# Loading, turning and masking the first two chunks of a windowed attention with FFN in another way

## The chip, the cores and the metric

The kernel runs on one core of a Trainium2 chip. The metric is device time in microseconds (us) of one execution; the time before is 178.18 us, the median of 3 runs (177.92 to 179.19). One further execution was recorded by the hardware profiler, and every duration below is from it.

The engines are named as in the profile: PE (TensorE, matrix products; PEld is its weight load), DVE (VectorE), ACT (ScalarE), POOL (GpSimd) and SP (SyncE, which here only issues DMAs). Each works through its own instructions in order and waits for others by semaphores. 16 DMA engines move data; SP and Pool each feed them through a queue of their own.

## The reference, cut to what matters

```python
scores = q @ k.T / sqrt(64)               # q, k, v: (4 batches, 8 heads, 768 tokens, 64)
keep   = is_sink | in_window              # first 4 tokens, or the 128 tokens up to this one
a      = softmax(where(keep, scores, -1e9))
x      = (a @ v), heads side by side      # (3072, 512)
h      = maximum(maximum(x @ w1, x @ w2), x @ w3)     # w1, w2, w3: (512, 768)
out    = h @ w_out                        # (3072, 512), float32
```

All inputs are float32; the kernel computes its products in bf16.

## The kernel before, in words

**Chunks.** The 3072 tokens are cut into 12 chunks of 256 (three to a batch). For each chunk: load K, Q, V; cast to bf16; turn K and Q so that the head dimension lies on the partitions; scores, exponentials, mask, sink scores; attention times V; normalise; turn the result; three FFN products with a running maximum; the output product; store. Heads are taken in four pairs (`p` = 0 to 3), the two heads of a pair are `a` = 0, 1. A group `g` is half of the heads, that is, two pairs. A token's number in its chunk is split as `(p i)`, so that a partition holds two tokens that follow each other; `n` is the half of the chunk of 128 keys.

**Order.** The order of instructions is written out by hand: each Python call appends its instructions to the engines' queues in the order of the calls (L408 to L613). The first chunks are written one by one, from chunk 3 on a loop runs (L561). The loop is full of FFN matmuls; the first 20 us, before the weights have landed, are not, and they are what the change rewrites.

**Loads.** `load` (L72) moves one of K, Q, V of a chunk from float32 in memory to a float32 tile (`k_raw`, `q_raw`, `v_raw`), in pieces of 512 bytes. At the start SP issues K and Q of chunk 0 in two halves of heads each, then V of chunk 0, then K, Q and V of chunk 1 (L131 to L134). `load_w` (L197) moves an FFN weight from float32 to bf16 through Pool's queue; W1 and W2 in halves of the model dimension, W3 in halves of the hidden one. Later loads are gated: a one-element copy on Pool writes the destination once something has landed, and the DMA waits for that copy (`after`, L485). Chunk 2's K and Q hang on the last half of W2, the output weight on W3.

**Turning.** `cast_qk` (L89) casts a group to bf16, and `turn` (L102) transposes its four 128x128 blocks on PE against the identity into one PSUM bank, which ACT (Q) or DVE (K of chunk 0) copies to `qT` and `kT`.

**Masks.** `masks` (L157) builds `msk` with 1 where a key is seen and 0 elsewhere; `msk0` is the same for the first chunk of a batch, with the sink tokens kept. `expo` (L232) takes the exponential of two PSUM banks on ACT and multiplies the pair by the mask on DVE (L239).

**Values.** `cast_v` (L97) casts a quarter of V to `vb`, which holds a column of ones as well, so that `av` (L284) yields the sum of the exponentials in a 65th column. `sink_k` and `sink_v` pick the four sink tokens' K and V out of a batch's first chunk, and `sink_score` (L241) scores against them.

**Filler and banks.** `warm(n)` (L143) issues n matmuls of 512 columns whose result nobody reads. PSUM has eight banks, which all PE results share in turn; a new result waits until the one that held its bank before has been read.

**First stretch.** Chunk 0's groups are cast by DVE (K) and ACT (Q), turned and scored; V's quarters are cast two by DVE and two by Pool; W1's two halves are issued by Pool behind these casts. K of chunk 1 is cast by ACT, Q by Pool, and both are turned between the `av` calls of chunk 0. Then chunk 0's result is turned (`xpose`), chunk 1 scored, and `ffn_h_half` (L351) does half a contraction of the first FFN product with each half of W1, mixed with `av` of chunk 1.

Of the kernel before, what the change touches and what calls it, by code (L numbers as in the profile page):

```python
# [9 lines left out]
F32 = mybir.dt.float32  # L10
# [6 lines left out]
def kernel(  # L17
# [31 lines left out]
    with tc.manual_schedule():  # L49
# [22 lines left out]
        def load(ci, what="kqv", gate=None, parts=1, only=None, eng=None):  # L72
# [4 lines left out]
            for w in what:  # L77
# [5 lines left out]
                for g in range(parts) if only is None else (only,):  # L83
# [3 lines left out]
                            .rearrange("h (p i) d -> p h (i d)", i=2))  # L87

        def cast_qk(ci, w, g, eng):  # L89
# [12 lines left out]
        def turn(ci, w, g, eng=None):  # L102

            pt = bank([128, 4, 128], BF16, "pt")
            x = bfs[ci, w]
            for i in range(4):
                y = x[:, 2 * g + i // 2, i % 2]
                nc.tensor.transpose(pt[:, i], y.rearrange("s a d -> s (a d)"), ident)  # L108
            if w == "q":
                nc.scalar.copy(  # L110
                    qT[ci % RING][:, 2 * g:2 * g + 2].rearrange("q p i n r -> q (p i) (n r)"), pt)
            else:
                (nc.scalar.copy if eng is nc.scalar else nc.vector.tensor_copy)(
                    kT[ci % RING][:, :, 2 * g:2 * g + 2].rearrange("q n p i r -> q n (p i) r"),
                    pt.rearrange("q x (n r) -> q n x r", r=64))
# [17 lines left out]
        load(0, "v")  # L133
        load(1)  # L134

# [18 lines left out]
        msk = const.tile([128, 2, 4, 128], BF16, name="msk")  # L154
        msk0 = const.tile([128, 2, 3, 128], BF16, name="msk0")

        def masks():  # L157
# [52 lines left out]

        def score(ci, pairs):
            b, c = divmod(ci, CPB)
            kc, qc = kT[ci % RING], qT[ci % RING]
            lo = 0 if c else 1
            sts = {p: [bank([128, 4, 128], F32, "st") for a in range(2)] for p in pairs}
            for p in pairs:
                st = sts[p]
                for s, x, n, q0, q1 in ((0, kT[(ci - 1) % RING], 1, 0, 1), (1, kc, 0, 0, 2),
# [3 lines left out]
                    for a in range(2):  # L222
# [4 lines left out]
                            rhs=qc[hp, p, :, q0:q1].rearrange("q i n r -> q n i r"),  # L227
                            start=True, stop=True)
                e = work.tile([128, 2, 4, 128], BF16, tag="e", bufs=2 * NP, name="e_sb")
                es[ci, p] = e, st  # L230

# [9 lines left out]
        def sink_score(ci):  # L241
# [4 lines left out]
            for p in range(NP):  # L246
# [4 lines left out]
                    start=True, stop=True, tile_position=(0, 32 * p))  # L251
            e = work.tile([128, 2, 128], BF16, tag="e_sink", bufs=2, name="e_sink")
            nc.scalar.activation(e, st, AF.Exp, scale=scale)  # L253
            es[ci, "sink"] = e

# [13 lines left out]
        def av_open(ci, pairs=range(NP)):  # L269
# [3 lines left out]
            if c:  # L273
                for t in range(2):
                    for p in pairs:
                        hp = slice(32 * p, 32 * p + 32)
                        nc.tensor.matmul(  # L277
                            os_[ci, p][:, t], lhsT=es[ci, "sink"][hp, t], rhs=vs[b % 2][hp],
                            start=(t == 0), stop=False, skip_group_check=True,
# [129 lines left out]
        masks()  # L409
        sink_init()  # L410
        cast_qk(0, "k", 0, nc.vector)
        cast_qk(0, "q", 0, nc.scalar)
        turn(0, "k", 0)
        turn(0, "q", 0)
        warm(3)
        score(0, (0, 1))
        cast_qk(0, "k", 1, nc.vector)
        cast_qk(0, "q", 1, nc.scalar)
        turn(0, "k", 1)
        expo(0, 0)  # L420
        warm(2)
        turn(0, "q", 1)
        warm(2)
        score(0, (2, 3))
        for i in range(2):
            cast_v(0, 0, i, nc.vector)
            cast_v(0, 1, i, nc.gpsimd)
        expo(0, 1)
        expo(0, 2)
        expo(0, 3)  # L430
        load_w(0, a1=2)
        load_w(0, a0=2)
        for g in range(2):
            cast_qk(1, "k", g, nc.scalar)
        for g in range(2):
            cast_qk(1, "q", g, nc.gpsimd)
        warm(3)
        av_open(0)
        av(0, 0)
        av(0, 1)  # L440
        turn(1, "k", 0, nc.scalar)
        av(0, 2)
        turn(1, "k", 1, nc.scalar)
        av(0, 3)
        warm(2)
        for g in range(2):
            turn(1, "q", g)
        sink_v(0)
        xpose(0, 0, nc.vector)
        xpose(0, 1, nc.vector)  # L450
        score(1, (0, 1))
        sink_k(0)
        load_w(1, a1=2)
# [4 lines left out]
        load_w(2, 0, d_ff // 2)  # L458
        load_w(2, d_ff // 2, d_ff)
        expo(1, 0)  # L460
        sink_score(1)
        expo(1, 1)
        score(1, (2,))
        score(1, (3,))
        expo(1, 2)
        expo(1, 3)
        ffn_h_half(0, 0)
        ffn_h_half(0, 1, (0,))
        av_open(1, (0, 1))
# [180 lines left out]
```

## Time and profile before

| | us |
|---|---|
| median of 3 runs | 178.18 (177.92 to 179.19) |
| the profiled execution | 178.1 |
| its span, first to last instruction | 176.4 |
| PE busy | 167.6 (95%) |
| DVE busy | 116.0 (66%) |
| ACT busy | 93.4 (53%) |
| Pool busy | 66.3 (38%) |

Times in a timeline count from the span's start. A row gives start, length, engine, source line, operation, what is written and read (partitions x elements), and how often; in brackets the idle time of the engine before it and what ended that. A row with several instructions runs from the first one's start to the last one's end, and ends of matmuls are modelled. A few more rows of the first 20 us:

```profile
1.26 3.58 PE L148 MATMUL warm<-wz 128*128 128x512 bf16 x8 [1.26 <-DVE wz L137]
...
7.13 0.62 ACT L94 CAST q_bf<-q_raw 128x512 bf16<-128x512 f32 x1 [0.78 <-DMA q_raw<-in_q_dram]
...
9.02 1.17 DVE L98 CAST vb<-v_raw 64x512 bf16<-64x512 f32 x2
...
10.62 1.56 POOL L200 DMA_DIRECT2D w<-in_moe_w_dram  x2
...
12.28 1.10 ACT L113 COPY kT<-pt 128x512 bf16<-128x512 bf16 x2
```

The DMA engines are busy from about 2 us on, throughout the first 40 us.

### The profile page before, as it was taken

To read this page: it belongs to the slowest core of one execution; us is meant where nothing else is said; L and a number is where in the kernel's file an instruction comes from. 1 tells how busy PE (TensorE), PEld (TensorE's weight loads), DVE (VectorE), ACT (ScalarE), POOL (GpSimd) and SP (SyncE) were. 2 spreads that over 40 slices of the span, in tenths; PEclk is the share of its full clock that TensorE was granted. 3 is DMA by queue.
4 is the path that set the end of the run, shared out by engine and by line. 5 is a ranking of instruction groups with operands and counts; after the bars stand their busy time and mean duration, and the time that the engine had idled before them with its cause. 6 is when DMAs were issued, how large, how long until landed. Compare 5 with 4: busy or idle time off the path is not lost.

```text
span 176.4 us, 4623 instructions
## 1 busy us (share of the span) xinstructions
PE 167.6 (95%) x1851; PEld 126.9 (72%) x1864; DVE 116.0 (66%) x260; ACT 93.4 (53%) x186; POOL 66.3 (38%) x120
## 2 busy tenths in 40 slices
PE   7879799999999999999999999999999999999992
PEld 2446588965787688687697687686796796796871
DVE  4499863859489468578388396397396496493441
ACT  3698734387773832933834924923726726722221
POOL 6089243077996065282271390480370000000000
PEclk9999999999999999999999999999999999999998
DMA  5999999999998999994995997996998903203203
GB/s 145 276 287 215 200 243 246 280 272 287 334 240 218 230 235 226 274 295 113 268 250 152 288 173 208 307 177 172 304 194 192 188 0 63 119 4 59 119 2 119
DMA packets 68341, 35.16 MB, mean 199 GB/s; under 512 B 27616, under 2 KB 66656, under 8 KB 68320
## 3 DMA queue, kind: packets, MB, share of 16 engines
q1 hardware_dynamic: 65104, 31.14, 77.1%
q0 software_dynamic: 3072, 3.67, 11.5%
q8 instruction: 14, 0.23, 0.5%
q10 hardware_dynamic: 144, 0.07, 0.1%
q14 instruction: 7, 0.06, 0.1%
HBM read 25.17 MB, written 6.29 MB: 178 GB/s over the span
## 4 chain that ended last, share of the span: by engine, by line
PE 84%; DMA 8%; DVE 3%; POOL 1%; SPq 1%; issue 1%; DVEq 0%; POOLq 0%
PE h_ps L338 49%; PE y_ps L381 18%; PE o L295 6%; PE st L224 5%; DMA w<-in_moe_w_dram 4%; DMA v_raw<-in_v_dram 3%; PE h_ps L362 2%; DVE h_sb L347 2%; PE o L277 1%; SPq L84 1%; PE pt L108 1%; POOL vb L98 1%; PE sk L247 1%; PE xt L314 1%; DVE x_sb L303 1%
## 5 line engine op out<-in xcount | busy, mean ns | idle before, releaser
L338 PE MATMUL h_ps<-xT,w 128*128 128x256 bf16 x816 | 97.2, 273 | 0.0
L338 PEld LDWEIGHTS <-w 128*128 128x128 bf16 x816 | 77.1, 98 | 10.8 <-issue 0.3
L347 DVE TENSOR_TENSOR h_sb<-h_sb,h_ps 128x512 bf16<-128x512 bf16 (+1 forms) x79 | 46.8, 615 | 15.9 <-PE h_ps L338 13.3
L239 DVE TENSOR_TENSOR e_sb<-e_sb,msk 128x1024 bf16<-128x1024 bf16 (+1 forms) x48 | 33.8, 714 | 31.7 <-ACT e_sb L237 31.5
L237 ACT ACTIVATE e_sb<-st 128x512 bf16<-128x512 f32 (+1 forms) x96 | 47.0, 577 | 6.1 <-PE st L224 6.1
L345 ACT CAST h_sb<-h_ps 128x512 bf16<-128x512 f32 x33 | 19.4, 588 | 33.3 <-PE h_ps L338 32.8
L98 POOL CAST vb<-v_raw 64x512 bf16<-64x512 f32 x44 | 28.0, 636 | 15.5 <-DMA v_raw<-in_v_dram 13.4
L381 PE MATMUL y_ps<-wo,h_sb 128*128 128x512 bf16 (+2 forms) x144 | 32.4, 361 | 0.7
L94 POOL CAST k_bf<-k_raw 128x512 bf16<-128x512 f32 x20 | 14.2, 735 | 40.1 <-issue 31.3
L381 PEld LDWEIGHTS <-h_sb 128*128 128x128 bf16 x156 | 14.3, 97 | 14.9 <-issue 1.3
L303 DVE TENSOR_TENSOR x_sb<-o,rc 128x256 bf16<-128x256 f32 x48 | 20.4, 424 | 1.6
L386 ACT COPY y_sb<-y_ps 128x512 f32<-128x512 f32 (+1 forms) x24 | 13.9, 586 | 11.8 <-PE y_ps L381 9.6
L295 PE MATMUL o<-vb,e_sb 128*128 128x65 bf16 x352 | 18.3, 194 | 0.5 <-POOL vb L98 0.2
L295 PEld LDWEIGHTS <-e_sb 128*128 128x128 bf16 x352 | 15.9, 98 | 2.8 <-issue 0.5
L224 PE MATMUL st<-qT,kT 64*128 64x128 bf16 (+1 forms) x256 | 13.4, 237 | 0.7 <-ACT qT L110 0.4
L94 POOL CAST q_bf<-q_raw 128x512 bf16<-128x512 f32 x18 | 12.6, 729 | 2.3 <-DMA q_raw<-in_q_dram 2.0
L224 PEld LDWEIGHTS <-kT 64*128 64x128 bf16 x256 | 9.1, 94 | 4.5 <-issue 2.2
L253 ACT ACTIVATE e_sink<-sk 128x256 bf16<-128x256 f32 x8 | 3.1, 384 | 15.8 <-PE sk L247 15.8
L300 DVE RECIPROCAL rc<-o 128x4 f32<-128x4 f32 x48 | 8.3, 173 | 0.1
L148 PE MATMUL warm<-wz 128*128 128x512 bf16 x19 | 6.8, 483 | 1.3 <-DVE wz L137 1.3
L362 PE MATMUL h_ps<-xT,w 128*128 128x256 bf16 x48 | 6.2, 273 | 1.3 <-DMA w<-in_moe_w_dram 1.2
L110 ACT COPY qT<-pt 128x512 bf16<-128x512 bf16 x8 | 4.5, 587 | 3.7 <-PE pt L108 3.6
(58 smaller groups left out, 63.8 us busy)
## 6 DMA issues: line engine op xcount, KB each, us to landing
v_raw<-in_v_dram SPq DMA_DIRECT2D x11, 512.0 KB, 7.0
k_raw<-in_k_dram SPq DMA_DIRECT2D x11, 512.0 KB, 5.2
q_raw<-in_q_dram SPq DMA_DIRECT2D x11, 512.0 KB, 6.4
out_dram<-y_sb SPq DMA_DIRECT2D x11, 512.0 KB, 3.3
w<-in_moe_w_dram POOLq DMA_DIRECT2D x6, 384.0 KB, 7.6
wo<-in_moe_w_out_dram POOLq DMA_DIRECT2D x1, 768.0 KB, 9.0
k_raw<-in_k_dram SPq DMA_DIRECT2D x2, 256.0 KB, 3.7
q_raw<-in_q_dram SPq DMA_DIRECT2D x2, 256.0 KB, 4.0
```

Source lines behind the costliest of these rows:

```text
L94: f(x[:, 2 * g:2 * g + 2].rearrange("q p i a d -> q p a i d"), y[:, 4 * g:4 * g + 4].rearrange("q (p a) i d -> q p a i d", a=2))
L98: eng.tensor_copy(vb[ci % RING][64 * i:64 * i + 64, n, :, 0:D], raws[ci, "v"][64 * n:64 * n + 64, :, i])
L224: nc.tensor.matmul(st[a][:, s:s + q1 - q0].rearrange("q n (i r) -> q n i r", i=2), lhsT=x[hp, n, p].rearrange("q i r -> q (i r)"), rhs=qc[ ...
L237: nc.scalar.activation(e[:, a, lo:], st[a][:, lo:], AF.Exp, scale=scale)
L239: nc.vector.tensor_mul(e[:, :, lo:], e[:, :, lo:], msk0 if lo else msk)
L295: nc.tensor.matmul(o[:, t, a], lhsT=e[:, a, s], rhs=vb[cv % RING][:, n, 2 * p + a], start=first, stop=True, skip_group_check=True)
L303: nc.vector.tensor_mul(xs[ci][:, :, p], o[:, :, :, 0:D], rc.unsqueeze(3).to_broadcast([128, 2, 2, D]))
L338: nc.tensor.matmul(hp[:, f].rearrange("q (i t r) -> q i t r", i=2, t=2), lhsT=w_sb[wi][:, ds, fb * 128:fb * 128 + 128], rhs=xTs[ci][:, :, ...
L345: nc.scalar.copy(dst, hp)
L347: nc.vector.tensor_max(dst, dst, hp)
L381: nc.tensor.matmul(yp, lhsT=hs[ci][:, fb, t * 128:(t + 1) * 128], rhs=wo[:, fb, d0:d1], start=(fb == 0), stop=(fb == FB - 1))
L386: nc.scalar.copy(ys[ci][:, t, d0:d1], yp)
```

## The change

K and Q of chunk 1 are no longer loaded as float32 by SP. Pool issues both with a cast to bf16 on the way (`load16`), each partition taking 16 tokens of one head, which is 4 KB of memory in one piece; a one-element copy on Pool gates the first of them behind the first turned K of chunk 0. V of chunk 1 is issued by Pool too, after Pool's cast of chunk 0's last Q. In the new layout a partition is (token block, head), so a plain transpose does not serve; `turn16` instead multiplies by `pick`, which holds columns of the identity: 16 matmuls of 64 columns for one of the two tokens `i`, into the upper or lower 64 partitions by head, then one ACT copy.

The last group of Q of chunk 0 is cast by Pool (before: ACT), and its turned form copied by DVE (before: ACT). For chunk 0's pairs 2 and 3 the mask is no product on DVE any more: PE first writes `add0` (0 where a key is seen, -1e30 elsewhere) into the bank by a product with the identity, and the scores are added to it. V of chunk 0 is cast three quarters by DVE and one by Pool. Three `warm(2)` go (two in chunk 0, one ahead of the turning of chunk 1's Q). Chunk 1's scores move ahead of the turning of chunk 0's result, and `av` of chunk 1 is mixed with the FFN halves in another order.

```diff
+        def load16(ci, w, gate=None):
+            b, c = divmod(ci, CPB)
+            x = bf2[w][ci % 2].rearrange("q p i a d -> q (p i a) d")
+            bfs[ci, w] = x
+            if gate is not None:
+                gate(x[0:1, 0, 0:1])
+            nc.gpsimd.dma_start(
+                out=x.rearrange("q j d -> q (j d)"),
+                in_={"k": k, "q": q}[w][b, :, c * 256:c * 256 + 256]
+                    .rearrange("h (g j) d -> g h (j d)", j=16))
+
+        def turn16(ci, w, i):
+            pt = bank([128, 512], F32, "pt16")
+            dims = "(n p g j)" if w == "k" else "(p n g j)"
+            y = pt.rearrange(f"q {dims} -> q p n g j", n=2, p=NP, g=8)
+            for j in range(8):
+                for a in range(2):
+                    nc.tensor.matmul(
+                        y[64 * a:64 * a + 64, :, :, :, j], lhsT=bfs[ci, w][:, 2 * j + i],
+                        rhs=pick[:, a].rearrange("q p (n g) -> q p n g", n=2),
+                        start=True, stop=True, tile_position=(0, 64 * a))
...
-        load(1)
...
+        def score_open(ci, pairs, add=False):
+            for p in pairs:
+                st = [bank([128, 4, 128], F32, "st") for a in range(2)]
+                if add:
+                    for a in range(2):
+                        nc.tensor.matmul(st[a][:, 1:4], lhsT=ident, rhs=add0,
+                                         start=True, stop=False, skip_group_check=True)
...
+        nc.gpsimd.tensor_copy(pick, ident.rearrange("q (g p a) -> q a p g", p=NP, a=2))
+        nc.gpsimd.tensor_scalar(add0, msk0[:, 0], BIG, -BIG, ALU.mult, ALU.add)
...
         turn(0, "q", 0)
+        load16(1, "k", lambda x: nc.gpsimd.tensor_copy(x, kT[0][0:1, 0, 0, 0, 0:1]))
+        load16(1, "q")
         warm(3)
         score(0, (0, 1))
         cast_qk(0, "k", 1, nc.vector)
-        cast_qk(0, "q", 1, nc.scalar)
+        cast_qk(0, "q", 1, nc.gpsimd)
+        load(1, "v", eng=nc.gpsimd)
         turn(0, "k", 1)
         expo(0, 0)
-        warm(2)
-        turn(0, "q", 1)
-        warm(2)
-        score(0, (2, 3))
-        for i in range(2):
-            cast_v(0, 0, i, nc.vector)
-            cast_v(0, 1, i, nc.gpsimd)
-        expo(0, 1)
-        expo(0, 2)
-        expo(0, 3)
+        expo(0, 1, mul=False)
+        score_open(0, (2,), True)
+        turn(0, "q", 1, nc.vector)
+        score_open(0, (3,), True)
+        score(0, (2, 3), True)
+        expo(0, 1, exp=False)
+        expo(0, 2, mul=False)
+        expo(0, 3, mul=False)
+        for n, i, eng in ((0, 0, nc.vector), (0, 1, nc.vector), (1, 0, nc.vector),
+                          (1, 1, nc.gpsimd)):
+            cast_v(0, n, i, eng)
         load_w(0, a1=2)
+        sink_k(0)
         load_w(0, a0=2)
-        for g in range(2):
-            cast_qk(1, "k", g, nc.scalar)
-        for g in range(2):
-            cast_qk(1, "q", g, nc.gpsimd)
         warm(3)
         av_open(0)
         av(0, 0)
+        turn16(1, "k", 0)
         av(0, 1)
-        turn(1, "k", 0, nc.scalar)
+        turn16(1, "k", 1)
+        turn16(1, "q", 0)
         av(0, 2)
-        turn(1, "k", 1, nc.scalar)
+        turn16(1, "q", 1)
         av(0, 3)
-        warm(2)
-        for g in range(2):
-            turn(1, "q", g)
         sink_v(0)
+        score(1, (0, 1))
+        sink_score(1)
         xpose(0, 0, nc.vector)
         xpose(0, 1, nc.vector)
-        score(1, (0, 1))
-        sink_k(0)
...
+        score(1, (2, 3))
         expo(1, 0)
-        sink_score(1)
+        expo_sink(1)
         expo(1, 1)
-        score(1, (2,))
-        score(1, (3,))
         expo(1, 2)
         expo(1, 3)
         ffn_h_half(0, 0)
-        ffn_h_half(0, 1, (0,))
         av_open(1, (0, 1))
         av(1, 0)
+        ffn_h_half(0, 1, (0,))
         av(1, 1)
         ffn_h_half(0, 1, (1,))
+        ffn_h_half(0, 1, (2,))
         av_open(1, (2, 3))
         av(1, 2)
-        ffn_h_half(0, 1, (2,))
+        ffn_h_half(0, 0, (0,), 1)
         av(1, 3)
-        ffn_h_half(0, 0, wi=1)
+        ffn_h_half(0, 0, (1, 2), 1)
         ffn_h_half(0, 1, (0,), 1)
         xpose(1, 0)
```

More of the change, by code (lines that the diff above doesn't have):

```diff
@@ L87, in load @@
                             .rearrange("h (p i) d -> p h (i d)", i=2))
+        def load16(ci, w, gate=None):
[18 more added lines that the diff above has]
+                        start=True, stop=True, tile_position=(0, 64 * a))
+            if w == "q":
+                nc.scalar.copy(qT[ci % RING][:, :, i].rearrange("q p n r -> q p (n r)"),
+                               pt.rearrange("q (p x) -> q p x", p=NP))
+            else:
+                nc.scalar.copy(kT[ci % RING][:, :, :, i].rearrange("q n p r -> q (n p) r"),
+                               pt.rearrange("q (x r) -> q x r", r=64))
         def cast_qk(ci, w, g, eng):
@@ L109, in turn @@
             if w == "q":
-                nc.scalar.copy(
+                (nc.vector.tensor_copy if eng is nc.vector else nc.scalar.copy)(
                     qT[ci % RING][:, 2 * g:2 * g + 2].rearrange("q p i n r -> q (p i) (n r)"), pt)
@@ L155 @@
         msk0 = const.tile([128, 2, 3, 128], BF16, name="msk0")
+        BIG = 1e30
+        add0 = const.tile([128, 3, 128], BF16, name="add0")
+        pick = const.tile([128, 2, NP, 16], BF16, name="pick")
         def masks():
@@ L209, with score @@
         es = {}
-        def score(ci, pairs):
+        def score_open(ci, pairs, add=False):
[5 more added lines that the diff above has]
+                                         start=True, stop=False, skip_group_check=True)
+                es[ci, p] = work.tile([128, 2, 4, 128], BF16, tag="e", bufs=2 * NP,
+                                      name="e_sb"), st
+        def score(ci, pairs, add=False):
             b, c = divmod(ci, CPB)
@@ L214, in score @@
             lo = 0 if c else 1
-            sts = {p: [bank([128, 4, 128], F32, "st") for a in range(2)] for p in pairs}
+            if not add:
+                score_open(ci, pairs)
             for p in pairs:
-                st = sts[p]
+                st = es[ci, p][1]
                 for s, x, n, q0, q1 in ((0, kT[(ci - 1) % RING], 1, 0, 1), (1, kc, 0, 0, 2),
@@ L227, in score @@
                             rhs=qc[hp, p, :, q0:q1].rearrange("q i n r -> q n i r"),
-                            start=True, stop=True)
-                e = work.tile([128, 2, 4, 128], BF16, tag="e", bufs=2 * NP, name="e_sb")
-                es[ci, p] = e, st
+                            start=not add, stop=True, skip_group_check=add)
         def expo(ci, p, exp=True, mul=True):
@@ L252, in sink_score, with expo_sink @@
             e = work.tile([128, 2, 128], BF16, tag="e_sink", bufs=2, name="e_sink")
+            es[ci, "sink"] = e, st
+            if ci > 1:
+                expo_sink(ci)
+        def expo_sink(ci):
+            e, st = es[ci, "sink"]
             nc.scalar.activation(e, st, AF.Exp, scale=scale)
-            es[ci, "sink"] = e
         def sink_v(b):
@@ L277, in av_open @@
                         nc.tensor.matmul(
-                            os_[ci, p][:, t], lhsT=es[ci, "sink"][hp, t], rhs=vs[b % 2][hp],
+                            os_[ci, p][:, t], lhsT=es[ci, "sink"][0][hp, t], rhs=vs[b % 2][hp],
                             start=(t == 0), stop=False, skip_group_check=True,
```

## The prediction

> **What bounds the kernel now.** The page comes first: TensorE (PE) is busy 167.6 of 176.4 us, and the slices say where it is not.
>
> ```profile
> span 176.4 us, 4623 instructions
> ...
> PE   7879799999999999999999999999999999999992
> ...
> POOL 6089243077996065282271390480370000000000
> ```
>
> Only the first four slices (17.6 us) and the last hold idle PE time. From then on this change alters no work, so all that counts is how early PE becomes dense. The chain of waits says what decides that now:
>
> ```profile
> 2.96 5.97 DMA v_raw<-in_v_dram
> ...
> 9.06 0.86 POOL vb L98
> ...
> 9.97 0.70 POOL vb L98
> 10.67 0.78 POOL w L200
> 11.44 7.63 DMA w<-in_moe_w_dram
> ...
> 19.12 0.61 PE h_ps L362 x4
> ...
> 23.97 0.45 PE xt L314 x8
> ```
>
> Columns are start, length, what. V of chunk 0 lands, Pool casts it, Pool issues the second half of W1, and that half ends PE's last long idle time at 19.12. From there to the transposes of chunk 1's attention (23.97), and on to the end, PE is full (4.85 of 4.85 us busy in that stretch). The start of those transposes is my milestone: both kernels have done exactly the same work by then, so an earlier milestone is an earlier end. Before it, the timeline shows the work that now waits for weights:
>
> ```profile
> 5.45 0.42 DVE L113 COPY kT<-pt 128x512 bf16<-128x512 bf16 x1 [0.49 <-PE pt L108]
> ...
> 9.04 0.51 PE L224 MATMUL st<-qT,kT 64*128 64x256 bf16 x8 [0.41 <-ACT qT L110]
> ...
> 14.93 0.62 PE L224 MATMUL st<-qT,kT 64*128 64x128 bf16 x12
> ...
> 16.50 1.47 PE L362 MATMUL h_ps<-xT,w 128*128 128x256 bf16 x12
> ```
>
> Scores of chunk 0's second half start at 9.04, of chunk 1 at 14.93; twelve FFN matmuls follow at 16.50, then 1.15 us of nothing. So W1 is late by 1.15 us, and a change that brings it early wins that much only if scores of chunk 1 do not come later.
>
> **Part 1: the transfers.** Removed from SP's queue: K, Q and V of chunk 1 (issued at 3.50 to 8.72; nothing stands behind them there until 22.93). Added to Pool's queue: K and Q with the cast, 128 rows of 4 KB each, behind a one-element copy that waits for VectorE's first turned K (ends 5.87). Queued behind that wait on Pool: both issues, the cast of chunk 0's last Q, V's issue, one V cast, all weights. One-element copies on Pool take 0.18, with 0.30 before the issue that follows (the W_out gate): first issue at 6.4. A weight half's issue takes 0.72 to 0.84; two end at 7.9. The Q cast (part 2) follows to 8.65, V's issue takes 0.90, the V cast 0.75, so W1's first half is issued at about 10.4 (10.62 now), the second, with the sink copies (0.45) between, at 11.7 (11.44).
>
> Do weights still arrive sooner? They stand in one queue behind 1.05 MB of K, Q and 0.52 MB of V. Weights move at about 200 GB/s in bf16, so 400 read; 512-byte packets at 290. K and Q: 2.6 us (3.6 at the slower rate); V: 1.8; W1: 3.9. From 7.5 that puts all of W1 at 15.8 to 16.8, and 1 us for the tail leaves 17.8 against 19.07. What needs it comes at 18.6 below, so waiting for weights ends; that slack is 0.8 us. W2 follows 2 us per half, at about 18.8 to 21.8, needed from 21.
>
> **Part 2: chunk 0's last Q.** ScalarE casts it at 7.13 and copies it turned; that goes to Pool (0.60 by its own Q casts, 1.08 at worst) and VectorE (0.42 for 0.59). Pool reaches it at 7.9, while VectorE masks pair 0: I take 0.75, so 8.65. Transposes 0.4, copy 0.42, signals: scores of pairs 2, 3 at 9.6 instead of 9.04. The late end is 10.0, the early one 9.2.
>
> **Part 3: masks by TensorE.** `add0` and `pick` are two Pool instructions under 0.6 us each, in a Pool that idles 5.37 us there; without that cover they would delay the gate. Four identity matmuls of 384 columns (0.16 each) fill PE gaps left by two removed pairs of filler. Removed: two mask products of 0.59 on VectorE. ScalarE's four exponentials take 1.72, and end at 11.6 (11.3 now).
>
> **Part 4: V of chunk 0.** VectorE now does three casts instead of two, after the copy of Q (9.54) and pair 1's mask (10.13): 0.42 to 0.57 each, so 11.6 (11.4 to 12.4 with the late end of part 2; 11.0 at best). All of attention-times-V now stands behind this; today its first matmuls go at 10.25. This is the new critical place.
>
> **Part 5: turning chunk 1.** Sixteen transposes (55 ns each dense, 0.9 us) become 64 matmuls of 64 columns that form two halves of the array's columns. No row is that. Nearest: the 65-column attention matmuls, 16 in 0.59 (37 ns), and the sink-V ones on quarter columns, 8 in 0.18 (22 ns). I take 30; 22 and 37 stay as ends, and 55 as a far end. PE's chain from 11.6: 0.13, four turns of 0.47, two pairs of 0.22 between: 14.05. Then ScalarE's last copy (0.2 signal, 0.58, 0.07): the scores of chunk 1 start at T = 14.9, practically as today (14.93). Ends: 11.0 with 22 ns gives 13.7; 12.4 with 37 ns gives 16.2. The four ScalarE casts and copies before (1.2 + 2.2 us) shrink to four copies, which removes ScalarE from the way; Pool's Q casts (1.16) go as well.
>
> **Part 6: from T to the milestone.** Scores 0.62, sink 0.22, transposes 0.45. The last bank of pairs 2, 3 is freed by the sink exponential: ScalarE starts at T+0.43, two exponentials of 0.52 and 0.39 give T+1.9, so these scores end at T+2.2. Twelve FFN matmuls 1.31. VectorE has two copies, two casts and the first mask by T+3.9: some 0.25 of wait. Then the same 4.85 us of work as after 19.12. Milestone T + 8.6. It equals 23.97 at **T = 15.4**: the point from which the change loses.
>
> **Sum.** 15.4 - 14.9 = 0.5 us earlier. After the milestone PE is full for both; chunk 2's K and Q hang on W2's last half, which also lands earlier (22.7 now), and chunk 2 is turned at 33.8 with its casts done by 31.8. The profiled execution took 178.1 (span 176.4 and 1.7 around it), the median is 178.18, so I forecast **177.7**. Parts 1 and 4 carry it: over a microsecond of weight wait goes, but half comes back as the chain Pool, TensorE, VectorE, TensorE, ScalarE. With the ends of T: 176.5 to 179.0.
>
> **Rivals.** *All low ends hold.* T = 13.7, and the 0.25 wait for masks vanishes too: 1.9 us gained, 176.2. For it: VectorE's two K casts took 0.42 each where Pool was idle, and quarter-column matmuls did go at 22 ns. Against: Pool runs beside all three V casts (0.57 each when it did).
>
> *Pool is late.* The six weight issues took 718 to 837 ns although VectorE was 97% busy in that stretch, so VectorE hardly holds them up. But casts of V on both engines at once took 0.75 on Pool and 0.57 on VectorE, against 0.61 and 0.42 alone: they do hinder each other. If each of the two issues waits out one VectorE instruction of 0.42, T is 15.7 and the time 178.5. [...]
>
> *Slower: the array's clock falls.* At the start eight fillers are 0.43 apart (3.58 us for eight); the three at 5.56 take 0.81 together, half of that each. So PE has a slow rate that it leaves after some 4 us of work, though the granted clock reads 1.00 in both. The change removes fillers and leaves PE thin from 7.2 to 11.6: about 2.7 us of work in 4.4. If the slow rate returns there, 64 turning matmuls cost 53 ns instead of 30 (+1.5), 24 attention ones +0.4, and score and sink +0.8: 2.7 late, less the 0.5 gain, 180.4. It decides when PE's work between 7.2 and 11.6 is too thin to hold the rate. Against: today's 10 to 12 is half empty (0.59, 0.51), 17.97 to 19.12 wholly, and the next matmuls are fast (four in 0.61). [...]
>
> **How the numbers follow.** My forecast 0.55, low ends 0.18, Pool late 0.14, slow rate 0.13. About 1% (1.8 us) is what a measurement of this kernel can tell from no change. Forecast and Pool late lie within it: same 0.69. Low ends count as faster, 0.18; the slow rate as slower, 0.13. The range goes from a little under the low-end rival (175.9) to the late end of T with 0.3 of spread (179.3) and leaves out the slow rate.
>
> **What would show it.** Right: no PE wait on a weight before the milestone; K of chunk 1 issued by Pool at 6.3 to 6.6; the Q cast done at 8.4 to 9.0; VectorE's third V cast ending at 11.2 to 12; sixteen turning matmuls in 0.35 to 0.6; the first chunk 1 scores at 14.9, the milestone at 23.5. Wrong: turning matmuls over 50 ns, a wait for W1, T under 14 or over 16, or a new idle stretch of PE after the milestone, which I priced at nothing.

## The result, and the profile after

The changed kernel takes 180.18 us (median of 22 runs, 178.34 to 182.75); the kernel before takes 178.04 in the runs beside it (177.12 to 181.03). The ratio is 1.0087, with a 95% interval of 1.0060 to 1.0115. That is slower by 0.9%, not faster, and the predicted 177.7 is missed with its whole range (175.9 to 179.3). In ten of the 22 runs, the profiled execution (182.75) among them, the granted clock is 0.986 to 0.991 and the time 181.4 or more, so the ratio leaves these ten out, and the profile shows a larger loss than the ratio does.

The page of the changed kernel, the lines that answer to those of before: span, PE's busy share in 40 slices, PE's granted clock (the last line is the clock of before).

```profile
span 181.0 us, 4719 instructions
...
PE   7679899999996999999999999999999999999991
...
PEclk9999999999999699999999999999999999999998
...
PEclk9999999999999999999999999999999999999998
```

The head is little thinner than before (7679 against 7879; filler was taken out of it). But there is a 6 in the thirteenth slice (54.3 to 58.8 us), where before had 9, and in the fourteenth the granted clock falls to 0.6. Both lie 30 us behind the last instruction that the change touches. The chain of waits (start, length, what) tells both halves:

```profile
8.07 0.98 POOL q_bf L124
9.06 0.36 POOL v_raw L84
...
9.98 0.94 POOL vb L128
10.92 0.65 POOL w L233
...
12.26 8.53 DMA w<-in_moe_w_dram
...
20.84 0.61 PE h_ps L409 x4
...
25.25 0.45 PE xt L361 x8
...
54.60 4.52 DMA qT<-q_bf
59.12 0.14 issue
59.25 0.29 PE sk L289 x4
...
60.56 4.36 PE y_ps L428 x12
```

The prologue is the one that was forecast, Pool, then W1, then FFN, only later: W1's second half lands at 20.79 instead of 19.07, and the milestone is at 25.25 instead of 23.97. Then a row that before's chain does not have: the DMA transposes of chunk 4's Q, issued at 54.60, land 4.52 us later. The timeline shows PE standing there (in brackets the idle time before the row and what ended it):

```profile
57.00 0.25 PE L309 MATMUL sv<-vb,sel 128*32 128x65 bf16 x8
59.25 0.29 PE L289 MATMUL sk<-qT,ks 128*32 128x256 bf16 x4 [2.01 <-DMA qT<-q_bf]
...
60.56 4.36 PE L428 MATMUL y_ps<-wo,h_sb 128*128 128x512 bf16 x12
```

In before the same four sink scores begin at 55.80 without any wait:

```profile
55.72 0.25 PE L262 MATMUL sv<-vb,sel 128*32 128x65 bf16 x8
55.80 0.28 PE L247 MATMUL sk<-qT,ks 128*32 128x256 bf16 x4
```

The output matmuls that follow in the changed kernel take 4.36 us; chunk 0's twelve take 2.59 in the same chain. Two rows of the changed kernel by stretch say why. The columns are the stretch and its length, then busy time of PE, PEld, DVE, ACT and POOL with instructions, granted clock, DMA share and GB/s:

```profile
60.00:62.00 2.00, 1.98 (x20) 0.95 (x15) 0.69 (x1) 1.97 (x4) 0.00 (x0) 0.61 1.06 215
62.00:64.00 2.00, 2.00 (x6) 0.71 (x5) 0.69 (x1) 0.64 (x2) 0.00 (x0) 0.54 1.15 292
```

So in this execution the wait is paid a second time, in clock. From chunk 5's sink scores to the end of the span the two kernels then take the same 107 us (176.4 - 69.49 and 181.0 - 74.00): nothing is lost or won after that.

### The profile page after: what moved, and what is told of

Read it like the earlier page. It is cut to its first block, busy times and chain, and to the rows that moved or that the text cites. A ratio compares the mean times of both kernels' runs of the same rounds, so it can differ in the third digit from the quotient of the medians.

```text
span 181.0 us, 4719 instructions
## 1 busy us (share of the span) xinstructions
PE 170.4 (94%) x1910; PEld 128.6 (71%) x1910; DVE 116.3 (64%) x260; ACT 91.6 (51%) x182; POOL 66.3 (37%) x124
## 4 chain that ended last, share of the span: by engine, by line
PE 84%; DMA 7%; POOL 4%; DVE 2%; issue 1%; POOLq 0%; DVEq 0%
PE h_ps L385 48%; PE y_ps L428 19%; PE o L342 6%; PE st L268 5%; DMA w<-in_moe_w_dram 5%; DMA qT<-q_bf 2%; PE h_ps L409 2%; PE pt L138 1%; PE o L324 1%; PE sk L289 1%; POOL q_bf L124 1%; POOL vb L128 1%; PE xt L361 0%; POOL k_bf L96 0%; DVE h_sb L394 0%
## 5 line engine op out<-in xcount | busy, mean ns | idle before, releaser
L385 PEld LDWEIGHTS <-w 128*128 128x128 bf16 x816 | 77.1, 98 | 10.7 <-issue 0.3
L281 DVE TENSOR_TENSOR e_sb<-e_sb,msk 128x1024 bf16<-128x1024 bf16 (+1 forms) x46 | 33.0, 729 | 32.7 <-ACT e_sb L279 32.6
L428 PE MATMUL y_ps<-wo,h_sb 128*128 128x512 bf16 (+2 forms) x156 | 34.8, 375 | 0.1
L128 POOL CAST vb<-v_raw 64x512 bf16<-64x512 f32 x43 | 27.3, 636 | 13.1 <-DMA v_raw<-in_v_dram 9.4
L124 POOL CAST k_bf<-k_raw 128x512 bf16<-128x512 f32 x20 | 13.5, 699 | 39.1 <-DMA k_raw<-in_k_dram 38.9
L428 PEld LDWEIGHTS <-h_sb 128*128 128x128 bf16 x156 | 14.9, 100 | 16.1 <-issue 3.4
L433 ACT COPY y_sb<-y_ps 128x512 f32<-128x512 f32 (+1 forms) x24 | 13.8, 585 | 12.4 <-PE y_ps L428 9.6
L268 PE MATMUL st<-qT,kT 64*128 64x128 bf16 (+1 forms) x256 | 12.9, 237 | 0.6 <-ACT qT L113 0.2
L124 POOL CAST q_bf<-q_raw 128x512 bf16<-128x512 f32 x17 | 10.8, 663 | 5.0 <-DMA q_raw<-in_q_dram 5.0
L177 PE MATMUL warm<-wz 128*128 128x512 bf16 x14 | 5.2, 524 | 1.3 <-DVE wz L166 1.3
L409 PEld LDWEIGHTS <-w 128*128 128x128 bf16 x48 | 4.2, 98 | 1.6 <-DMA w<-in_moe_w_dram 1.0
```

The lines of the kernel that those rows point to most:

```text
L128: eng.tensor_copy(vb[ci % RING][64 * i:64 * i + 64, n, :, 0:D], raws[ci, "v"][64 * n:64 * n + 64, :, i])
L268: nc.tensor.matmul(st[a][:, s:s + q1 - q0].rearrange("q n (i r) -> q n i r", i=2), lhsT=x[hp, n, p].rearrange("q i r -> q (i r)"), rhs=qc[ ...
L281: nc.vector.tensor_mul(e[:, :, lo:], e[:, :, lo:], msk0 if lo else msk)
L385: nc.tensor.matmul(hp[:, f].rearrange("q (i t r) -> q i t r", i=2, t=2), lhsT=w_sb[wi][:, ds, fb * 128:fb * 128 + 128], rhs=xTs[ci][:, :, ...
L409: nc.tensor.matmul(hp[:, f].rearrange("q (i t r) -> q i t r", i=2, t=2), lhsT=w_sb[wi][:, ds, fb * 128:fb * 128 + 128], rhs=xTs[ci][:, :, ...
L428: nc.tensor.matmul(yp, lhsT=hs[ci][:, fb, t * 128:(t + 1) * 128], rhs=wo[:, fb, d0:d1], start=(fb == 0), stop=(fb == FB - 1))
```

## The experiments

Four landmarks are read from each timeline: T, the first scores of chunk 1; the milestone, the first row of the transposes of chunk 1's attention (23.80 in before by the timeline, where the chain has 23.97); y0, the first output matmul of chunk 0 (37.94); and the first sink scores of chunk 4 (55.80). From y0 to those scores, PE has 17.86 us of work in before without a gap. In the profile of the changed kernel the four stand at 15.98, 25.09, 39.22 and 59.25: 1.3 us of its loss are there at y0, 2.2 more at chunk 4's scores, and 1.1 more, the clock's, at chunk 5's (74.00 against 69.49). All runs of before lay between 176.47 and 181.21, its medians between 177.69 and 178.12.

**Is it the prologue?** Two runs each take one delay out of the changed kernel.

```diff
-        load16(1, "k", lambda x: nc.gpsimd.tensor_copy(x, kT[0][0:1, 0, 0, 0, 0:1]))
+        load16(1, "k")                             # e1_no_gate
...
-        cast_qk(0, "q", 1, nc.gpsimd)
+        cast_qk(0, "q", 1, nc.scalar)              # e2_q_by_act
```

> The changed kernel without the one-element gate copy: Pool issues K and Q of chunk 1 as soon as its constants are built, about 4.7 us instead of 6.83. Theory A (the change leaves the DMA engines short of work between 7.5 and 10.5 us, where they move some 100 GB/s, and everything behind in Pool's queue lands late by that): the second half of W1 lands 1.0 to 2 us earlier than its 20.8, PE waits for no weight, chunk 2's K is issued before 23.5 (24.85 now), and the time falls by 1 to 2 us. Theory B (the chain Pool cast, turned Q, three V casts on VectorE sets the scores of chunk 1, transfers do not matter): W1 lands within 0.5 us of where it does now, and only what Pool's earlier Q cast gives is gained, at most 1 us at the first score of chunk 1 (15.98 now).

> The changed kernel with the cast of chunk 0's last Q back on ScalarE. Theory B: the cast ends at about 7.8 instead of 9.06, scores of chunk 0's pairs 2 and 3 start 0.9 to 1.2 us earlier than 10.03, the first scores of chunk 1 at 14.8 to 15.3 instead of 15.98, and the time falls by 0.7 to 1.2 us. Theory A: V of chunk 1 is issued 1 us earlier and the weights with it, but K and Q still start at 6.8, so W1's second half still lands after 19.8, PE still waits for it, and the time falls by less than 0.6 us.

Measured: e1_no_gate 179.91 (ratio 1.0122, 1.0079 to 1.0165), e2_q_by_act 180.08 (1.0106, 1.0067 to 1.0144). Both did to the prologue what was meant: milestone 23.98 and 23.78, as in before, with no wait for W1. Both times stayed. PE waited 1.87 and 3.34 us for chunk 4's Q transposes instead. What the prologue gives is lost at chunk 4.

**Is it the queue ahead of those transposes?** On SP's queue V of chunk 5 stands directly before them. It was moved behind them in the changed kernel, in before, and together with e1_no_gate.

```diff
-        load(5)
+        load(5, "kq")
         cast(4)
         turn_dma(4, "k")
         turn_dma(4, "q")
+        load(5, "v")
```

> The changed kernel with V of chunk 5 issued by SP behind the DMA transposes of chunk 4's K and Q instead of ahead of them. Theory C (after the start, the lost time grows because chunk 4's transposes stand on SP behind late loads, and land 2 us after PE wants them, at 59.2): the transposes start at 47.6 instead of 50.4, PE does not wait at chunk 4's sink scores, no output matmuls run at half rate behind that wait, and the median falls by 1 to 3 us; the first 26 us are as they were. Rival (the wait is only a sign, PE would meet its next late transfer anyway): the wait goes from 57 us but a similar one appears behind it, and the time stays within 0.5 us.

> The kernel before with nothing but V of chunk 5 put behind chunk 4's K and Q transposes on SP's queue, as in e3_v5_behind. Theory C (chunk 4's Q transposes have no slack in the kernel before, but end in time; the swap is worth something only where they are late): within 0.5 us of before, 177.6 to 178.6, first scores of chunk 4 without a wait as before. Rival (the swap itself costs what e3_v5_behind was still behind before by, 1.1 us, because Pool then waits for V of chunk 5): 178.9 to 179.4. Second rival (the transposes are late enough in before to hide a gain): 177.0 to 177.5.

> e1_no_gate and e3_v5_behind together: K, Q of chunk 1 on Pool's queue without the gate, and V of chunk 5 behind chunk 4's transposes. If the ungated order loses only by the wait for chunk 4's Q transposes (1.9 us of PE in e1_no_gate, of which the swap takes all): 178.0 to 178.6. If the prologue's lost transfers come out at another place once that wait is gone: 179.0 to 179.5, as e3_v5_behind.

Measured: e3_v5_behind 179.26 (1.0066, 1.0039 to 1.0093), e5_before_v5_behind 177.79 (0.9987, 0.9950 to 1.0024), e6_no_gate_v5_behind 179.94 (1.0093, 1.0054 to 1.0132). The wait at chunk 4's scores is gone in all three, and before neither gains nor loses by the swap. What the changed kernel gains (1.0066 against 1.0087) lies inside the intervals, and e6 lies above both ranges that were expected. A new wait of 0.88 and 0.92 us stands before the next FFN in e3 and e6, and the transposes of chunk 3's attention output, which that FFN needs, took 5.4 us in both (3.2 in before, 3.6 in e5). The loss had moved to the next set of transposes.

**Which half of the change?** One run is before with K and Q of chunk 1 by `load16` and `turn16` alone (gated, V of chunk 1 on SP); the other is before with most of the rest: masks by TensorE, Q by Pool and VectorE, V casts three to one. V of chunk 1 through Pool and the new order of chunk 1's calls are in neither.

```diff
-        load(1)                                    # e4_kq_alone
+        load(1, "v")
...
+        load16(1, "k", lambda x: nc.gpsimd.tensor_copy(x, kT[0][0:1, 0, 0, 0, 0:1]))
+        load16(1, "q")
...
-        turn(1, "k", 0, nc.scalar)
+        turn16(1, "k", 0)
...
-        cast_qk(0, "q", 1, nc.scalar)              # e7_masks_alone
+        cast_qk(0, "q", 1, nc.gpsimd)
...
+        score_open(0, (2,), True)
+        turn(0, "q", 1, nc.vector)
+        score_open(0, (3,), True)
+        score(0, (2, 3), True)
```

> The kernel before with one part of the change: K and Q of chunk 1 in bf16 through Pool's queue behind the gate, turned by the 64 matmuls. V of chunk 1 stays on SP, the last Q cast and its copy on ScalarE, V of chunk 0 two casts each, masks on VectorE, order as before. Theory A: the gate alone costs; W1's second half lands at 19.5 to 21 and the time is 0 to 1.5 us above the kernel before. Theory B: the chain of chunk 0 is as before (scores of pairs 2, 3 at about 9.0), so the first scores of chunk 1 start within 0.6 us of 14.93 and the time is within 0.5 us of the kernel before.

> The kernel before with the other half of the change alone: last Q of chunk 0 cast by Pool and copied by VectorE, masks of pairs 2 and 3 by TensorE, V casts of chunk 0 three to VectorE and one to Pool; K, Q, V of chunk 1 stay on SP's queue in fp32 and are turned as before. Theory (the loss is all in the transfers of chunk 1): chunk 4's transposes start within 0.3 us of before's 47.78 and 52.09 and the time is 177.5 to 178.5. Rival (the reordered engines of the prologue cost by themselves): over 178.8.

Measured: e4_kq_alone 179.37 (1.0093, 1.0062 to 1.0124), e7_masks_alone 178.09 (0.9996, 0.9968 to 1.0024). K and Q alone cost as much as the whole change; 0.6 us of it is there at y0 (38.55).

**The empty stretch, the gate, or the casting transfer?** In the changed kernel the DMA engines moved only 103 GB/s from 8 to 10 us (290 in before), while K and Q waited for their gate. I held that bytes not moved there made chunk 4 late. Three runs try it: V of chunk 1 put into the gap; the gate without the cast; the cast without the gate.

```diff
         load(0, "v")
+        load(1, "v")                               # e8_v1_by_sp, in after
...
-        load(1, "v", eng=nc.gpsimd)
...
-        load(1)                                    # e9_gate_fp32, in before
...
         turn(0, "q", 0)
+        load(1, gate=lambda x: nc.gpsimd.tensor_copy(x, kT[0][0:1, 0, 0, 0, 0:1]))
...
-        load16(1, "k", lambda x: nc.gpsimd.tensor_copy(x, kT[0][0:1, 0, 0, 0, 0:1]))
+        load16(1, "k")                             # e10_bf16_no_gate, in e4
```

> The changed kernel with V of chunk 1 issued by SP right behind V of chunk 0 instead of by Pool at 9 us, so that the DMA engines have 512 KB in the stretch from 7.5 to 10.5 us where they moved 90 to 130 GB/s. Theory (bytes not moved in that hole are what makes chunk 4's transposes late): no hole, chunk 4's Q transposes start near 52.1 instead of 54.6, no wait at its first scores, time 178.0 to 178.6. Rival (the lateness comes from the order of the queues after 25 us): transposes at 53.5 or later, time 179.4 to 180.2. K of chunk 1 behind V can also be later and T with it: up to 1 us on T, which the theory prices at nothing unless W1 waits for it.

> The kernel before with the gate alone: K, Q and V of chunk 1 stay in fp32 on SP's queue and are cast and turned as before, but their issue waits for chunk 0's first turned K (near 6 us), by three one-element copies of Pool. With e4_kq_alone (gate and bf16 by Pool: 179.37) and e10_bf16_no_gate it separates the gate from the bf16 transfer. Theory G (what costs is the stretch that the gate leaves empty): DMA rate of the stretch from 8 to 10 us under 150 GB/s, first scores of chunk 1 a us or more later than 14.93, chunk 4's Q transposes at 53.5 us or later, 179.3 to 180.5. Theory H (what costs is the casting transfer on Pool's queue): 177.8 to 178.5.

> The kernel before with K and Q of chunk 1 in bf16 by Pool's queue and turned in sixteens as in e4_kq_alone, but without the gate, so that they are issued near 4.7 us; V of chunk 1 on SP. Theory G: no empty stretch, so 177.8 to 178.5, chunk 4's Q transposes near 52.1. Theory H: V of chunk 0 lands 1 to 2 us later than before's (the casting transfers share the engines with it), the weights of W1 are no sooner, and the time is 179.0 to 180.0, as e1_no_gate and e4_kq_alone.

Measured: e8_v1_by_sp 180.08 (1.0108, 1.0063 to 1.0153). The stretch was full (279 GB/s), and the wait at chunk 4 was gone, but K of chunk 1 now came behind V: T at 16.76, milestone at 24.89, which is 1.1 us of its loss. e9_gate_fp32 178.06 (1.0018, 0.9996 to 1.0039); e10_bf16_no_gate 179.74 (1.0101, 1.0055 to 1.0146). By their times the casting transfer seemed to be what costs; e12 below has no such transfer. The gate costs nothing that can be measured. The theory of the empty stretch falls by e4 and e10, which moved 280 and 208 GB/s from 8 to 10 us and lose 0.9 and 1.0% (e9 moved 266, so it tests the gate and not the stretch). In e10 PE reached y0 at 37.64, 0.3 us sooner than in before, the transposes were issued nearly as early (52.44 against 52.09), and PE still waited 1.39 us for them.

What told the kernels apart was the landing time. Chunk 4's Q transposes took 4.5 to 4.6 us in after, e1, e2, e4 and e10, and 3.1 to 3.2 in before, e7, e8 and e9. When they were issued is a second term: in e7 and e9 that was at 54.08 and 53.58, and their profiles show PE waiting 0.69 and 1.05 us for transposes that took no longer than in before. The DMA view of just that stretch, from issue to landing, cut into 40 slices (digits: mean busy tenths of the 16 engines; then GB/s; then the queues with packets, MB and share), first for the kernel before:

```profile
DMA  9993933351899999999999999999999995939395
GB/s 138 115 102 79 89 69 72 72 63 36 182 300 280 300 290 274 77 221 221 221 230 214 201 214 207 204 227 207 214 181 181 227 758 185 685 158 685 158 632 211
...
q1 hardware_dynamic: 1889, 0.71, 108.0%
...
qT<-q_bf SPq DMA_TRANSPOSE x1, 3.1
```

and for the changed kernel:

```profile
DMA  9900000004999999999000001001001999979939
GB/s 55 25 18 18 23 14 18 18 18 80 285 290 290 227 349 272 272 270 84 0 0 0 0 2 9 7 9 11 9 9 27 270 290 290 535 293 580 544 145 471
...
q1 hardware_dynamic: 1734, 0.68, 103.4%
q8 instruction: 1, 0.02, 1.5%
...
qT<-q_bf SPq DMA_TRANSPOSE x1, 4.5
```

Twelve slices of 0.113 us, 1.4 us in all, move nothing, or 2 to 27 GB/s, between 56.7 and 58.1, and in the same stretch there is a packet that before does not have: one of queue q8, "instruction". It begins at 56.2, half a microsecond ahead of the dead stretch. In before's whole run the page counts 14 such packets with 0.23 MB, 16 KB each. I read them as fetches of PE's code, by the counts: PE has 1864 weight loads and as many matmuls in before, 266 instructions for each packet; the changed kernel has 1910 of each and 15 packets, 255 for each; and 115 to 139 matmuls, each with its weight load, run between one packet and the next.

`turn16` makes 64 matmuls, and with them 64 weight loads, of 16. With these some 90 instructions ahead of them, the packets come 3 to 4 us earlier: those near 38.5, 49 and 58.5 us in before, e7 and e9 stand near 35, 45.5 and 55 (54.0 to 55.8) in e4, e8 and e10. The one at 55 falls on chunk 4's Q transposes (in e8 at 55.7, when they are ending: issued at 52.70, landed 3.2 us later).

**The number of instructions alone.** The sharp test adds 48 pairs of weight load and matmul to before, with no cast, no transfer and no new order: filler of 64 columns in place of filler of 512 columns that takes as long. Two more runs keep K and Q in bf16 and add pairs until the sum is 256 (250) instructions, about what the counts give for one packet of 16 KB (255 and 266), so that the packets should stand again where before has them.

```diff
-        def warm(n):
+        def warm(n, m=0):
...
+                for _ in range(m):
+                    nc.tensor.matmul(pw[0:64, 0:64], lhsT=wz[:, 0:64], rhs=wz[:, 0:64],
+                                     start=True, stop=True)
...
-        warm(8)                                    # e12, in before; two warm(3) to (1, 13), one warm(2) to (1, 6)
+        warm(4, 25)
...
-        warm(8)                                    # e13, in after; two warm(3) to (0, 19)
+        warm(4, 25)
...
+        warm(0, 29)
         turn(0, "q", 1, nc.vector)
...
-        warm(8)                                    # e14, in e10; two warm(3) to (0, 19), two warm(2) to (0, 14)
+        warm(4, 25)
```

> The kernel before with 48 more pairs of weight load and matmul on TensorE, and nothing else: some of the 512-column warm-up matmuls of the prologue are replaced by 64-column ones that take as long together. K and Q of chunk 1 in sixteens brings as many pairs more (1864 weight loads before, 1912 in e10_bf16_no_gate). Theory F (TensorE's instructions are fetched 16 KB at a time by the DMA engines, one packet near 38.5, 49 and 58.5 us in before and near 34.5, 45.5 and 55 us in every kernel with the sixteens; the one near 55 falls on chunk 4's Q transposes, which take 4.5 to 4.8 us to land there and 3.1 to 3.3 where no packet falls on them): the packets come 3 to 4 us sooner, chunk 4's Q transposes take 4.4 or more, PE waits at chunk 4's first scores, 178.8 to 180.0. Rival (the casting transfers, not the number of instructions): 177.7 to 178.3, transposes 3.1 to 3.4.

> The changed kernel with 82 more pairs of weight load and matmul in the places of the warm-up matmuls and in PE's idle stretch at 8 us, so that TensorE's stream is 256 instructions (16 KB) longer than before's and the fetches fall where they fall in before. Theory F: packets near 49 and 58.5 us, chunk 4's Q transposes 3.1 to 3.4 us, no or under 1 us of wait at its first scores: 177.8 to 178.8, against 179.7 to 180.2 of the changed kernel. Rival: as the changed kernel, 179.5 to 180.3, with a wait near 2 us.

> e10_bf16_no_gate (K and Q of chunk 1 in bf16 and in sixteens, 179.74) with 77 more such pairs, for 250 instructions more than before. Theory F: as before or a little sooner, since chunk 0's outputs began 0.3 us sooner in e10_bf16_no_gate: 177.4 to 178.3. Rival: 179.3 to 180.

Measured: e12_before_48_more 179.47 (1.0091, 1.0053 to 1.0129). The kernel before, with nothing but 48 more pairs and its milestone at 23.91, loses what the change loses. Its DMA view from issue to landing, and its timeline:

```profile
DMA  9111170000999999999000000001000999999939
...
q8 instruction: 1, 0.02, 1.6%
...
qT<-q_bf SPq DMA_TRANSPOSE x1, 4.6
```

```profile
58.34 0.29 PE L250 MATMUL sk<-qT,ks 128*32 128x256 bf16 x4 [1.71 <-DMA qT<-q_bf]
```

The same dead stretch, the same packet, the same kind of wait. The transposes were also issued later than in before (53.64 against 52.09); why is open. e14_bf16_no_gate_phase 178.43 (1.0050, 1.0020 to 1.0079, against 1.0101 of e10): transposes 3.1 us, packets near 49.5 and 58, no wait in the profile. e13_after_phase 180.17 (1.0126, 1.0092 to 1.0159) missed: the wait is gone, but the filler itself cost 1.7 us of the prologue (T 17.63), and a packet at 51.5 now met the transposes (issued at 52.01), which took 4.4 us; PE did not wait because it came later itself (y0 at 39.90). The filler cost so much because until 10.9 us these small matmuls took 59 ns each (19 of them at 12.25 took 0.79 us, 42 ns each):

```profile
9.26 1.71 PE L179 MATMUL warm<-wz 128*64 128x64 bf16 x29
10.90 0.40 PE L138 MATMUL pt<-ident,q_bf 128*128 128x128 bf16 x4
```

That run settles nothing about the time of the changed kernel. So the pairs were put elsewhere: the output matmuls of chunks 0 and 1 in four times 128 columns (72 more pairs), the first filler in 256 columns (8 more).

```diff
-            for fb in range(FB):
-                nc.tensor.matmul(yp, lhsT=hs[ci][:, fb, t * 128:(t + 1) * 128], rhs=wo[:, fb, d0:d1],
-                                 start=(fb == 0), stop=(fb == FB - 1))
+            n = (d1 - d0) // (4 if ci < 2 else 1)
+            for c in range(0, d1 - d0, n):
+                for fb in range(FB):
+                    nc.tensor.matmul(yp[:, c:c + n], lhsT=hs[ci][:, fb, t * 128:(t + 1) * 128],
+                                     rhs=wo[:, fb, d0 + c:d0 + c + n],
+                                     start=(fb == 0), stop=(fb == FB - 1))
...
-        warm(8)
+        warm(16, 256)
```

> The changed kernel with 80 more pairs of weight load and matmul, put where they take no time of their own: the output matmuls of chunks 0 and 1 in 128 instead of 512 columns (72 more), the first warm-up in 256 columns (8 more); 252 instructions more than before, so that from 46 us on the fetches stand where before has them. In e13_after_phase the wait at chunk 4's first scores was gone, but its additions cost 2 us of the prologue. Theory F: chunk 4's Q transposes 3.1 to 3.4 us, no wait at its first scores (or under 0.5), no run with a granted clock under 0.993, and what is left against before is the prologue's: 178.0 to 179.2. Rival (the wait has another cause): 179.5 to 180.3.

> e10_bf16_no_gate with the same 80 pairs (256 instructions, 16 KB, more than before). Chunk 0's outputs began 0.3 us sooner in e10_bf16_no_gate than in before; e14_bf16_no_gate_phase, which lost that in the prologue, was at 178.43. Theory F: 177.3 to 178.2. Rival: 179.2 to 180.

Measured: e15_after_phase_y, the changed kernel whole, 178.68 (1.0051, 1.0029 to 1.0073). e16_bf16_no_gate_phase_y 178.27 (1.0021, 0.9988 to 1.0054), against 1.0101 (1.0055 to 1.0146) of e10; its profile has transposes of 3.3 us and 0.33 us of wait. (e14 and e16 lie 0.1 above the ranges that were expected.) In e15 the same stretch of transposes, and the sink scores:

```profile
DMA  9222227115999999799999999999999999796979
...
q1 hardware_dynamic: 1792, 0.72, 97.3%
...
qT<-q_bf SPq DMA_TRANSPOSE x1, 3.2
```

```profile
55.84 0.25 PE L309 MATMUL sv<-vb,sel 128*32 128x65 bf16 x8
56.09 0.29 PE L289 MATMUL sk<-qT,ks 128*32 128x256 bf16 x4
```

No packet, no dead stretch, no wait.

**What is left.** Two runs combine terms: e11 is the changed kernel with the last Q cast by ScalarE and V of chunk 5 behind; e17 is e15 with that cast by ScalarE (the edits are those above).

> The changed kernel with the last Q of chunk 0 cast by ScalarE (e2_q_by_act: first scores of chunk 1 at 15.26) and V of chunk 5 behind chunk 4's transposes (e3_v5_behind): both terms that the study found, at once. If they add: the wait for chunk 4's Q transposes gone and the transposes of chunk 1's attention at 23.9, so 178.0 to 178.6, no better than before, because the kernel before has no wait in either place. If something else is left in the change that costs: 179.0 to 179.6, as e3_v5_behind. If a start 0.3 us earlier than before's in chunk 1 is kept to the end: 177.5 to 177.9.

> e15_after_phase_y (178.68) with the last Q of chunk 0 cast by ScalarE, which took 0.7 us off the first scores of chunk 1 in e2_q_by_act and was lost there in the wait at chunk 4. If that wait is gone with the fetches moved, part of it should now be kept: 177.6 to 178.3, as before or a little under. If the W1 weights set the start of chunk 0's outputs instead: 178.4 to 178.9, as e15_after_phase_y.

Measured: e11_act_and_v5 178.82 (1.0067, 1.0039 to 1.0094), a miss of its first expectation: chunk 4's scores did not wait, but the transposes of chunk 3's output, with a packet at 56.7, took 4.8 us. It is the case of e3 and e6 again: with V out of the way, the fetch meets the next transposes (in e3 a packet at 56.4, 0.6 us behind their issue; in e6 one at 54.2 that took 2.8 us, ahead of their issue at 56.46). e17_phase_y_act 178.15 (1.0018, 0.9992 to 1.0044), as before, with 0.62 us of wait left in its profile. So by the ratios the changed kernel is 0.9% above before, 0.5% with the fetches moved (e15), and 0.2% with the Q cast moved as well (e17). That makes the fetch some four tenths of the loss and Pool's cast of the last Q as much again, with a rest that cannot be told from nothing; the intervals of neighbouring steps overlap, so these shares are rough. No version is faster than before by more than can be measured.

All kernels but e13 sort by the number of PE's weight loads, as their pages give it (each stands for a matmul too; a record or so can be missing):

| weight loads | kernels | ratio to before |
|---|---|---|
| 1864 | e5, e7, e9 | 0.9987, 0.9996, 1.0018 |
| 1910 to 1912 | after, e1, e2, e3, e4, e6, e8, e10, e11, e12 | 1.0066 to 1.0122 |
| 1990 to 1992, most of them added to the output products | e15, e16, e17 | 1.0051, 1.0021, 1.0018 |
| 1989 to 1992, filler in the prologue | e14, e13 | 1.0050, 1.0126 |

What stays open: the trace gives the mean of the 16 DMA engines, so it is an inference that the transposes are spread over all of them and that a single engine with the packet holds them up. It fits the size: in slices of 0.5 us most packets fill 12 to 15% of 16 engines, 1.0 to 1.2 us of one engine, and the dead stretch is 1.4 us. Not every packet does this: in before one at 49.1 falls into chunk 4's K transposes, with V of chunk 5 in the queue ahead of them, and the engines go on at 225 GB/s or more. What decides it was not tried. That q8's packets here are PE's is inferred from the counts. And the 0.4 and 0.6 us by which the timed medians of e14 and e15 lie above their profiled executions (both have a span of 176.4, as before) were not tracked down. Every landing time and wait here is from one execution of its kernel, and e15's profiled execution is the shortest of its twelve.

## Why the prediction was wrong

**The step that failed** is in the sum: "After the milestone PE is full for both", and in the last paragraph "a new idle stretch of PE after the milestone, which I priced at nothing". It named the place of the loss and gave it no price. PE was full there in before, but with little slack: its sink scores of chunk 4 began 0.6 us after the transposes that they need had landed (52.09 + 3.1 against 55.80). In the changed kernel they took 1.4 us longer, and were issued 2.5 us later (54.60), of which 1.3 is the later y0; PE stood for 2.01 us, and the clock fell behind it. With 3.1 us to land, the wait would have been about 0.5 us (an estimate: 54.60 + 3.1 against 57.24, from which PE stood).

**The root is in part 5.** It priced 64 matmuls in place of 16 transposes by their time alone, 30 ns each. The time was right (from a group of 16 to the next row's start 0.44 to 0.58 us, 28 to 36 ns each, inside the bounds that were given). Their number was not considered at all, and the number is what the turning cost: e12 has the number without the matmuls' work, and costs the same 0.9%; e16, with the fetches moved, gives back most of e10's loss (1.0021 against 1.0101).

**Part 1**, "Do weights still arrive sooner?": no. Weights in one stream from 7.5 us at 400 GB/s did not happen. K's issue came at 6.83 rather than 6.4, because the first four transposes began at 5.21 (5.02 before) and took 0.61 us (0.40 before) and the copy behind them ended at 6.27. From 8 to 10 us the engines moved 103 GB/s. W1's second half, due by 17.8, landed at 20.79. In e3, whose prologue is the same, there is no wait for W1 and the milestone is 23.87; so this term varies from run to run, between nothing and 0.67 us of wait.

**Parts 2 to 4** were mis-sized by a little each, in one direction: the Q cast on Pool 0.99 instead of 0.75 (0.62 in e3), three V casts done at 12.25 instead of 11.6. T came at 15.98 (15.74 in e3 with the same prologue, 15.62 in e15 with the first filler in halves) instead of 14.9, so past the 15.4 at which the change was said to win nothing. e17, with the cast on ScalarE, has T at 15.37 and its milestone 0.3 us sooner than before's (23.50 against 23.80), and then the time of before; against e15 that cast is some 0.3 points of the loss. Part 6's length held: from T to the FFN 2.1 us, to the milestone 8.1 by the timeline's rows (8.3 by the chain's) where W1 was there, against 8.6. The early end of T is 13.8 by its own terms, not 13.7, which changes nothing here.

**The rivals.** Low ends: no. Pool late: the issues of K and Q took 0.71 and 0.53, less than assumed, and V's 0.92 against 0.90, so none was held up by the 0.42 of this rival; Pool was late by what it waited for and by its cast. Slower clock: its 180.4 lies near the measured 180.18 by luck. A slower rate exists, but not where I put it: the turning matmuls ran at 28 to 36 ns, and the rate fell at 60 us, behind a wait of 2.01 us. In e2 the clock fell as well, behind 3.34 us of waiting (a 5 and an 8 in its page's slices from 59.3 to 68.5 us), and in e1, behind 1.87, it did not (9 in every slice). That is one execution each, so no limit is shown.

## What to carry to other kernels

Count instructions, not only their time: in this kernel, one long unrolled stream, packets of the instruction queue pass through the same DMA engines as the data (15 of them, 0.6% of the 16 engines' span in the changed kernel's page), and 48 more small matmuls early on moved the packets behind them (in e12 those near 49 and 58.5 us of before to 46 and 55). When a local change costs time tens of microseconds later, compare the landing times of equal transfers in the two traces, look at their stretch for packets of the instruction queue, and test it with neutral instructions before blaming the change. And where an engine is full but begins its next work within a microsecond of its data's landing (0.6 us here), price that slack: here a milestone 1.1 and 1.3 us earlier than the changed kernel's, in e1 and e2, was worth nothing in time, and in the profile of the changed kernel the wait of 2.01 us was paid for twice, as the clock behind it read 0.61 and 0.54.

## What the hardware showed that was not expected

- Where a 16 KB instruction packet met a set of DMA transposes, the set took 4.4 to 4.6 us instead of 3.1 to 3.6 (Q of chunk 4), and 4.8 to 5.4 instead of 3.2 to 3.6 (attention output of chunk 3 in e3, e6 and e11 against before, e5 and e15). For 1.4 us the 16 engines moved 0 to 27 GB/s.
- Behind 2.01 us of PE waiting the granted clock read 0.61 and 0.54 in the two stretches from 60 to 64 us; twelve matmuls of 512 columns took 4.36 us instead of 2.59.
- With 64-column fillers in e13, PE was slow far into the prologue: 29 of them took 1.71 us at 9.3 us (59 ns each), 19 took 0.79 at 12.25 (42 ns each), and sixteen 64-column products of `turn16` took 0.64 at 14.2 (40 ns each); the granted clock reads 1.00 from 5 to 10 and from 12 to 16 us. In e12, with fewer of them, the first transposes already took 0.40 at 5.0 us. What decides it was not tried.
